# A linear-attention and MLP kernel: scores, masks and state updates of two chunks made side by side, in a new order of all steps

## The chip, the cores and the metric

The kernel runs on one core of a Trainium2 chip. The metric is the device time of one execution in microseconds (us), the median of several runs. A core has five engines that run side by side, each with its own list of instructions: TensorE (PE, with its weight loads shown as PEld), VectorE (DVE), ScalarE (ACT), GpSimd (POOL) and SyncE (SP), which here issues all the transfers. Engines wait for each other on semaphores. PE writes to PSUM, of which this kernel uses eight banks; everything else lies in SBUF.

## The reference

A recurrence over 768 tokens, for 4 batches of 8 heads of 48 channels, then a two-layer MLP with hardswish on the 3072 x 384 result.

```python
for t in range(S):                       # S = 768; state is B x H x 48 x 48
    state = alpha[:, :, t, :, None] * state + np.einsum('bhd,bhe->bhde', k[:, :, t], v[:, :, t])
    y[:, :, t] = np.einsum('bhd,bhde->bhe', q[:, :, t], state)
...
x = attn_out.transpose(0, 2, 1, 3).reshape(B * S, H * D)      # 3072 x 384
h = x @ w_in                                                  # 384 x 2048
relu6 = np.clip(h + 3.0, 0.0, 6.0)
g = h * relu6 / 6.0
return (g @ w_out).astype(np.float32)                         # 2048 x 384
```

The two weight matrices come as float64 and are turned to float32 on the chip.

## The kernel before

**Attention.** The tokens are cut into 24 chunks of 128, six for each batch. The 8 heads of a chunk lie as 4 pairs of two. A chunk goes through these steps, each with a short name that the order below uses, and a chunk number behind it:

- `la`, `lk`, `lq`, `lv` load alpha, k, q and v (L248, L271). `ta`, `tk`, `tq` turn them to channels by tokens: for chunks 0 to 5 on PE through PSUM (L282), from chunk 6 on with a DVE transpose of 32x32 blocks (L286); `ca` places alpha.
- `r` (L309, a scan, with the reciprocal of L313) is the product of the alphas from a token to the end of the chunk, `p` (L320) its counterpart from the start. `k` and `q` multiply by them (L332, DVE).
- `sc` (scores, L338 to L346) makes k by q in 32 matmuls: for each of 4 pairs, 2 halves of the chunk and 2 heads, a block of 64x64. The heads with a = 0 go to one PSUM bank, those with a = 1 to another, each using 256 of the bank's 512 columns. `m` (masked, L348 to L356) multiplies them by a triangular mask into the tile A: four DVE operations of 64x256. `qa` (L366, ACT) puts q itself into the other rows of A.
- `kb` and `ck` bring k back to tokens by channels: on PE up to chunk 7, later by a DVE transpose (`kt`, L391) and a trip through DRAM (`kw`, `kr`).
- `u` (update, L423 to L429) makes k by v in 32 matmuls (16 in a batch's last chunk), one PSUM bank for each half, 192 columns used. `sm` (L437, L439, DVE) adds it to the state; `st` (L409, POOL) decays the state; `sv` (L419, ACT) puts it into rows of v, so that `ya` and `yb` (attend, L455, 32 matmuls a chunk in 64 records) give masked scores by v and q by state added in one go. `cy` (L464, ACT) copies the result to xT.

**MLP.** Two chunks make a group of 256 tokens. Groups 0 and 1 run plain: first layer `f`, `fa`, `fb` (L478, L489), gate `fr` (ACT), hidden value `fg` (DVE), second layer `b` (L516). Groups 2 to 11 run with fewer products and more sums: `xc` (DVE) makes combinations of x, `M` (L600) 20 products, `n` (L606, ACT) keeps some of them, `o` (L537, L539, L541, DVE) adds them up, `e` (L494, ACT) and `h` (L498, DVE) make the hardswish; `s` (L647, L664, DVE) combines hidden values, `P` (L703) are seven products, `K` (ACT) keeps some, `G` (L719, DVE) adds up, `O` stores. `x` and `y` make the combinations of the weights that these products need.

**Weights.** 16 slices of 128x768: `w` loads one, `d1`, `d2`, `dx` (ACT), `d3` (DVE; L203 and L205, or L207, L208 and L210) and `d4` (POOL, L217) take the float64 words apart and together again.

**Idle fill.** `z` (L532) are matmuls on nothing needed, 29 in all.

**What sets the order.** Everything stands in one list of words in `run("""...""")` under a manual schedule: `sc.4.0.2` is scores of chunk 4 in the banks t0 and t2, `M.2.0.2` product 0 of group 2 in bank m2. Each engine, and SP with its transfers, executes its share of the list in that order; where two words meet in a bank or a tile, the later waits. There are four banks t0 to t3 for attention and four m0 to m3 for the MLP. The tiles A (two, by the parity of the chunk) and the quads, in which chunks from 6 on are loaded, are allocated once; the parts of the quads that no transfer fills are set by small POOL memsets (L257) in the loads of chunks 6 and 7.

The lines for A, the pads, the masks and the updates before:

```python
t = consts.tile([C, 2, H, HB], FP, tag=f"A{r}", name=f"A{r}")              # one for r = 0, one for r = 1
...
if j < FIRST + NQ:                                                          # in load_akq
    for o in (BLK, 3 * BLK):
        nc.gpsimd.memset(to[o : o + BLK, :, V - 1, D - BLK : BLK], 1.0)
```

Of the kernel before, what the change touches and what calls it, by code (L numbers as in the profile page):

```python
# [8 lines left out]
FP = mybir.dt.float32  # L9
# [4 lines left out]
ALU = mybir.AluOpType  # L14
# [3 lines left out]
def kernel(  # L18
# [42 lines left out]
    G = 2  # L61
# [32 lines left out]
    for r in range(NV):  # L94
        t = consts.tile([C, 2, H, 64], FP, tag=f"v{r}", name=f"v{r}")
        nc.gpsimd.memset(t, 0.0)
        vs.append(t)
    for r in range(2):
        t = consts.tile([C, 2, H, HB], FP, tag=f"A{r}", name=f"A{r}")
        nc.gpsimd.memset(t, 0.0)  # L100
        As.append(t)
# [145 lines left out]

    def load_akq(name, j):  # L248
# [6 lines left out]
        if j < FIRST + NQ:  # L255
            for o in (BLK, 3 * BLK):
                nc.gpsimd.memset(to[o : o + BLK, :, V - 1, D - BLK : BLK], 1.0)  # L257
# [80 lines left out]
    def scores(j, *at):  # L338
        sc = ps_t["sc", j] = [banks[i][:, 0 : NP * HB].rearrange("s (p t) -> s p t", p=NP)
# [28 lines left out]
    def last(j):  # L368
        return j % NC == NC - 1
# [52 lines left out]
    def update(j, *at):  # L422
        for b, i in enumerate(at):  # L423
            ps_t["u", j, b] = banks[i][:, 0 : NP * D].rearrange("r (p n) -> r p n", p=NP)
# [296 lines left out]
    def store2(g, i):  # L721
# [8 lines left out]
        "lq": lambda j: load_akq("q", j), "lv": load_v, "w": load_weight,  # L730
# [4 lines left out]
        "sc": scores, "m": masked, "qa": place_q, "kb": k_by_token, "ck": keep_k,  # L735
# [9 lines left out]
    def run(words):  # L745
        for word in words.split():
            name, *at = word.split(".")
            steps[name](*(int(x) for x in at))

    with tc.manual_schedule():  # L750
        run("""z.0.5 z.0.3 z.0.1 z.0.8 qa.0.0 w.0 d2.0 d3.0 la.0 ta.0.0 ca.0 r.0 lk.0 tk.0.1 k.0
               z.0.2 p.0 la.1 ta.1.2 lq.0 tq.0.3 ca.1 r.1 lk.1 lv.0.0 sv.0.0 d1.0 kb.0.0 ck.0 z.0.2
               u.0.2.1 sm.0.0 sv.0.1 q.0 qa.0.1 tk.1.0 k.1 p.1 z.0.2 sc.0.2.3 m.0 la.2 ta.2.0 ca.2
               dx.0 w.2 d2.2 kb.1.0 ck.1 lq.1 r.2 sm.0.1 st.1 tq.1.2 q.1 d3.2 z.0.3 d1.2 dx.2 lv.1.1
               u.1.3.1 sv.1.0 sm.1.0 p.2 sm.1.1 sc.1.0.2 m.1 ya.0.3 yb.0 cy.0 lq.2 w.1 d1.1 tq.2.1
               q.2 d4.2 lk.2 tk.2.3 k.2 fa.2.0 d4.0 st.2 sc.2.0.2 d2.1 d3.1 m.2 dx.1 d4.1 qa.1.1
               lk.3 la.3 ta.3.1 ca.3 la.4 fa.0.1 sv.1.1 w.3 r.3 ta.4.3 ca.4 r.4 tk.3.1 k.3 kb.2.0
               qa.1.0 d2.3 ya.1.2 yb.1 cy.1 fa.1.2 lq.3 ck.2 d1.3 p.3 d3.3 lv.2.2 u.2.3.2 sm.2.0
               d4.3 fb.2 tq.3.1 q.3 fb.1 qa.2.0 sm.2.1 sv.2.0 st.3 fr.0.2.0 fg.0.2 lk.4 tk.4.0
               sv.2.1 w.5 d2.5 k.4 d3.5 d1.5 qa.3.0 d4.5 qa.2.1 sc.3.1.3 m.3 w.6 d2.6 d1.6 d3.6 d4.6  # L760
               lv.3.0 lq.4 w.7 kb.3.2 fb.0 f.0.3.3 kb.4.0 ya.2.1 ck.3 u.3.3.2 sm.3.0 fr.0.3.1 fg.0.3
               fr.0.1.0 fg.0.1 qa.3.1 sv.3.0 sm.3.1 p.4 d2.7 sv.3.1 d1.7 d3.7 d4.7 f.0.5.0 fr.0.5.1
               fr.0.0.0 fg.0.5 fg.0.0 tq.4.3 ck.4 la.5 ta.5.2 f.0.6.3 ca.5 w.4 d2.4 ya.3.0 yb.3 cy.3
               fr.0.6.1 yb.2 cy.2 w.9 d2.9 q.4 qa.4.1 d1.4 d1.9 dx.4 la.6 w.8 d3.4 r.5 lk.5 w.10
               d3.9 p.5 ca.6 fg.0.6 d4.9 w.12 lq.5 lv.4.1 d2.8 d3.8 f.0.7.2 d1.8 st.4 d4.8 d4.4 w.11
               fr.0.7.0 fg.0.7 f.1.7.0 fr.1.7.1 fg.1.7 sc.4.0.2 m.4 f.1.1.1 fr.1.1.0 fg.1.1 f.1.3.3
               fr.1.3.1 d2.10 d1.10 tk.5.3 f.1.0.2 d2.12 d3.10 d4.10 w.13 fg.1.3 fr.1.0.0 fg.1.0 k.5
               d3.12 lq.6 f.1.6.0 f.1.2.1 u.4.1.0 sm.4.0 d1.12 d4.12 sv.4.0 qa.4.0 ya.4.2 fr.1.6.1
               fg.1.6 w.15 tq.5.3 fa.4.3 sv.4.1 d2.11 kb.5.1 d2.13 fr.1.2.0 f.1.4.2 fr.1.4.1 d1.11
               sm.4.1 q.5 r.6 d3.11 d3.13 fg.1.4 d4.11 lv.5.0 lk.6 tq.6 p.6 d2.15 d3.15 fg.1.2 d1.13  # L770
               d4.13 sc.5.0.3 yb.4 f.1.5.0 fr.1.5.1 fg.1.5 tk.6 m.5 b.1.0.2 fb.4 b.1.1 d1.15 d4.15
               st.5 y.5 w.14 la.7 lk.7 cy.4 d2.14 qa.5.1 ck.5 b.0.0.1 fr.0.4.0 d3.14 k.6 q.6 ca.7
               fg.0.4 d1.14 d4.14 x.0 y.1 y.10 b.0.1 y.0 y.2 u.5.2 P.1.0.0 K.1.0 qa.5.0 sv.5.0
               qa.6.1 P.1.1.3 b.0.2 b.1.2 kb.6.0 ya.5.3 y.6 s.1.0.0 sm.5.0 sv.5.1 G.1.0.0 tk.7
               s.1.1.1 s.1.2.3 x.1 yb.5 cy.5 b.1.3 sc.6.1.2 lv.6.2 ck.6 u.6.3.0 s.1.3.2 x.2 P.1.2
               b.0.3 K.1.1 y.7 s.1.4 s.1.5 y.11 y.3 r.7 xc.2.1 x.3 y.4 y.8 xc.2.3 k.7 xc.2.0 xc.2.4
               y.9 y.12 y.16 y.13 y.15 P.1.3.3 K.1.2 P.1.4 bo.1 P.1.5 xc.2.5 G.1.1.1 P.1.6 y.14 y.17
               y.19 xc.2.6 sm.6.0 G.1.2.2 y.20 M.2.0.2 lv.12.1 la.8 O.1.1 O.1.0 ca.8 y.18 y.21 y.23
               so.1 G.1.3.3 n.2.0.8 bo.0 lq.7 lv.7.0 O.1.2 m.6 xc.2.2 xc.2.10 xc.2.7 tq.7 r.8 p.7
# [153 lines left out]
```

## Time and profile before

| | us |
|---|---|
| median of 3 runs (533.48 to 533.62) | 533.5 |
| the profiled execution | 533.84 |
| its span, from the first to the last record | 531.8 |
| granted TensorE clock, mean | 1.00 |
| busy: PE, DVE, ACT, POOL | 522.2, 477.0, 257.4, 50.4 |

The profile is that of one execution. The 2.0 us by which its time exceeds the span lie around what the profiler records. The costliest groups on PE are the products of the second layer (L703: 121.7 + 91.5 us in 1232 records) and of the first (L600), on ACT the copies of L606 (63.6 us) and the gates of L494 (56.8 us), on DVE the hidden values of L498 (53.7 us in 80) and the sums of L537. The masks (L356) are 96 operations on DVE with 36.0 us, 0.413 each by duration. A row of the page or a view has: line, engine, operation, output and input, shape; then count, busy time and the mean of one. A matmul of float32 has more than one record.

### The profile page before, as it was taken

What the parts mean: (1) busy time and instruction counts of PE and PEld (TensorE: products, weight loads), DVE (VectorE), ACT (ScalarE), POOL (GpSimd) and SP (SyncE); (2) the same over time, 40 slices, a digit from 0 to 9 for tenths busy, and PEclk for the clock granted to TensorE, in tenths of its full rate; (3) what the DMA queues carried; (4) which work ended last, traced back from release to release, by engine and by line L of the source; (5) the groups of instructions that cost most, each with busy time, mean ns of one, the idle gap of its engine ahead of it and who ended that gap; (6) DMA issues with size and microseconds to landing.
All of it is one profiled execution on the core that took longest, in us unless ns stands there. A gap on an engine that the chain in (4) does not pass through costs nothing.

```text
span 531.8 us, 15143 instructions
## 1 busy us (share of the span) xinstructions
PE 522.2 (98%) x6306; PEld 496.9 (93%) x6306; DVE 477.0 (90%) x849; ACT 257.4 (48%) x503; POOL 50.4 (9%) x71
## 2 busy tenths in 40 slices
PE   7799999999999999999999999999999999999997
PEld 7698886789999999999999999999999999999997
DVE  6999989999999999999999999999999899496382
ACT  3889865212653553553544444642634544553340
POOL 5333425100000000000000000000000000000000
PEclk9999999999999999999999999999999999999999
DMA  9998887006615156254345356055364052100001
GB/s 173 218 254 247 211 231 156 18 2 149 155 31 118 30 125 139 49 137 100 89 107 118 90 123 143 18 134 111 92 138 105 10 110 44 44 2 2 15 16 37
DMA packets 124100, 54.40 MB, mean 102 GB/s; under 512 B 83328, under 2 KB 116864, under 8 KB 124032
## 3 DMA queue, kind: packets, MB, share of 16 engines
q1 hardware_dynamic: 124032, 53.44, 44.0%
q8 instruction: 49, 0.80, 0.7%
q14 instruction: 19, 0.16, 0.1%
HBM read 44.50 MB, written 8.91 MB: 100 GB/s over the span
## 4 chain that ended last, share of the span: by engine, by line
PE 81%; DVE 9%; ACT 3%; DMA 3%; POOL 2%; issue 1%; SPq 0%; DVEq 0%; POOLq 0%; ACTq 0%
PE m_ps L703 34%; PE m_ps L600 34%; PE m_ps L478 4%; PE t_ps L455 3%; PE t_ps L346 2%; PE t_ps L429 2%; DMA v<-in_v_dram 1%; DMA raw<-in_moe_w_out_dram 1%; DVE rings L647 1%; DVE R L309 1%; DVE raw L537 1%; ACT raw L186 1%; DVE g_sb L647 1%; ACT raw L191 1%; DVE w L537 1%
## 5 line engine op out<-in xcount | busy, mean ns | idle before, releaser
L606 ACT COPY g_sb<-m_ps 128x512 f32<-128x512 f32 x110 | 63.6, 584 | 123.7 <-PE m_ps L600 104.3
L703 PE MATMUL m_ps<-w,g_sb 128*128 128x192 f32 x704 | 121.7, 327 | 0.0
L703 PEld LDWEIGHTS m_ps<-w,g_sb 128*128 128x128 f32 x704 | 113.7, 190 | 0.4
L703 PE MATMUL m_ps<-rings,g_sb 128*128 128x192 f32 x528 | 91.5, 326 | 0.0
L703 PEld LDWEIGHTS m_ps<-rings,g_sb 128*128 128x128 f32 x528 | 85.4, 190 | 0.1
L600 PE MATMUL m_ps<-xc,w 128*128 128x128 f32 x640 | 82.8, 277 | 0.4 <-DVE w L541 0.4
L600 PEld LDWEIGHTS m_ps<-xc,w 128*128 128x128 f32 x640 | 77.5, 192 | 1.7 <-issue 0.6
L494 ACT ACTIVATE r<-g_sb,half 128x512 f32<-128x512 f32 x80 | 56.8, 722 | 33.1 <-DVE g_sb L541 12.1
L498 DVE SCALAR_TENSOR_TENSOR g_sb<-r,g_sb 128x512 f32<-128x512 f32 x80 | 53.7, 683 | 4.3 <-ACT r L494 3.9
L600 PE MATMUL m_ps<-xT,raw 128*128 128x128 f32 x400 | 52.5, 277 | 0.0
L600 PEld LDWEIGHTS m_ps<-xT,raw 128*128 128x128 f32 x400 | 48.6, 192 | 0.6
L409 POOL TENSOR_TENSOR st<-sm,R 128x192 f32<-128x192 f32 x20 | 12.9, 643 | 352.2 <-DVE sm L439 305.5
L647 DVE TENSOR_TENSOR g_sb<-g_sb 128x512 f32<-128x512 f32 (+1 forms) x55 | 41.9, 792 | 0.2
L600 PE MATMUL m_ps<-xT,w 128*128 128x128 f32 x320 | 42.0, 276 | 0.0
L600 PEld LDWEIGHTS m_ps<-xT,w 128*128 128x128 f32 x320 | 39.3, 192 | 0.1
L366 ACT COPY A<-q 48x256 f32<-48x256 f32 x88 | 35.6, 404 | 5.0 <-DVE q L332 3.8
L356 DVE TENSOR_TENSOR A<-t_ps,mask 64x256 f32<-64x256 f32 x96 | 36.0, 413 | 0.4
L478 PE MATMUL m_ps<-xT,w 128*128 128x256 f32 x144 | 32.8, 382 | 0.1
L600 PE MATMUL m_ps<-xc,raw 128*128 128x128 f32 x240 | 31.8, 276 | 0.0
L309 DVE TENSOR_TENSOR_SCAN R<-t,ones 128x516 f32<-128x516 f32 x24 | 29.6, 1235 | 1.0 <-ACT t L300 0.9
L478 PEld LDWEIGHTS m_ps<-xT,w 128*128 128x128 f32 x144 | 26.7, 190 | 3.8 <-POOL w L217 0.2
L600 PEld LDWEIGHTS m_ps<-xc,raw 128*128 128x128 f32 x240 | 29.6, 192 | 0.1
(104 smaller groups left out, 725.8 us busy)
## 6 DMA issues: line engine op xcount, KB each, us to landing
raw<-in_moe_w_out_dram SPq DMA_DIRECT2D x8, 768.0 KB, 5.3
raw<-in_moe_w_in_dram SPq DMA_DIRECT2D x6, 768.0 KB, 6.6
v<-in_v_dram SPq DMA_DIRECT2D x48, 96.0 KB, 3.1
out_dram<-oh SPq DMA_DIRECT2D x44, 96.0 KB, 1.7
far<-kq SPq DMA_DIRECT2D x64, 64.0 KB, 2.2
kb<-far SPq DMA_DIRECT2D x64, 64.0 KB, 2.1
aq<-in_alpha_dram SPq DMA_DIRECT2D x36, 96.0 KB, 2.7
qq<-in_q_dram SPq DMA_DIRECT2D x36, 96.0 KB, 2.5
```

The costliest lines, as they stand in the source:

```text
L309: nc.vector.tensor_tensor_scan(out=reverse(R, n - 1, n), data0=reverse(ax, n, n), data1=reverse(ones, n, n), initial=0.0, op0=ALU.mult, op ...
L356: nc.vector.tensor_tensor(out=to[:, a], in0=sc[a][half], in1=mask[half, half].unsqueeze(1).to_broadcast([HB, NP, HB]), op=ALU.mult)
L366: nc.scalar.copy(out=to[:, a], in_=Q_t[j][64 * a : 64 * a + D, :, half])
L409: nc.gpsimd.tensor_tensor(out=st, in0=sm, in1=R_t[j][:, :, 0:1].to_broadcast([C, NP, D]), op=ALU.mult)
L455: nc.tensor.matmul(y_of(j, (i + 1) // 2, p)[:, HB * b : HB * b + HB], vb[:, p, e : e + 32], A_t[j][:, b, 2 * p + a], start=(b == 0 and i = ...
L478: nc.tensor.matmul(h[:, f], w1[:, kk, o : o + C], xT_t[g][:, kk], start=(kk == 0), stop=(kk == KT - 1))
L494: nc.scalar.activation(out=to, in_=h, func=AF.Relu, bias=half, scale=1.0 / 6.0)
L498: nc.vector.scalar_tensor_tensor(out=to, in0=r, scalar=1.0, in1=h, op0=ALU.min, op1=ALU.mult)
L600: nc.tensor.matmul(acc[g][i][:, f * C : (f + 1) * C], spots[w][:, f * C : (f + 1) * C], x_of(g, x), start=(first and f == 0), stop=last, s ...
L606: nc.scalar.copy(out=slots[z], in_=acc[g][i])
L647: nc.vector.tensor_tensor(out=out, in0=in0, in1=in1, op=ALU.subtract)
L703: nc.tensor.matmul(to[g], a, rhs[:, f], start=(first and f == 0), stop=(last and f == HF - 1), skip_group_check=True)
```

## The change

From chunk 8 on (chunks 8 and 9, 10 and 11, ... 22 and 23) three steps take two chunks at a time:

- `sp` (scores_of_two) makes the scores of j and j + 1 in the same two banks: chunk j in columns 0 to 255, j + 1 in columns 256 to 511. The matmuls are the same.
- `mp` (masked_two) masks both with four DVE operations of 64x512 in place of eight of 64x256. For that the two tiles A become one tile `both`, whose two parts are still called As[0] and As[1].
- `up` (update_two) makes the updates of both chunks in the same banks, j in columns 0 to 191, j + 1 in columns 192 to 383. The matmuls are the same; the sums `sm` still go chunk by chunk.

Besides, the memsets on the quads leave `load_akq` and become a word of their own, `pd` (two of them, six memsets each), which stands near the beginning of the list. And the whole list of words is new: the place of nearly every step, and the bank that it uses.

```diff
+    both = consts.tile([C, 2, 2, H, HB], FP, tag="A", name="A")
     for r in range(2):
-        t = consts.tile([C, 2, H, HB], FP, tag=f"A{r}", name=f"A{r}")
-        nc.gpsimd.memset(t, 0.0)
-        As.append(t)
+        nc.gpsimd.memset(both[:, :, r], 0.0)
+        As.append(both[:, :, r])
...
+    def pad(r):
+        for name in "akq":
+            for o in (BLK, 3 * BLK):
+                nc.gpsimd.memset(quads[name, r][o : o + BLK, :, V - 1, D - BLK : BLK], 1.0)
...
-        if j < FIRST + NQ:
-            for o in (BLK, 3 * BLK):
-                nc.gpsimd.memset(to[o : o + BLK, :, V - 1, D - BLK : BLK], 1.0)
...
-    def scores(j, *at):
-        sc = ps_t["sc", j] = [banks[i][:, 0 : NP * HB].rearrange("s (p t) -> s p t", p=NP)
+    def scores_of_two(j, *at):
+        for c in range(2):
+            scores(j + c, *at, o=c * NP * HB)
+        ps_t["sp", j] = [banks[i] for i in at]
+
+    def masked_two(j):
+        sc = ps_t.pop(("sp", j))
+        for c in (j, j + 1):
+            A_t[c] = As[c % 2]
+        for b in range(2):
+            half = slice(HB * b, HB * b + HB)
+            to = both[half, b].rearrange("s c (p a) t -> s a (c p) t", a=2)
+            for a in range(2):
+                nc.vector.tensor_tensor(
+                    out=to[:, a], in0=sc[a][half].rearrange("s (n t) -> s n t", t=HB),
+                    in1=mask[half, half].unsqueeze(1).to_broadcast([HB, 2 * NP, HB]), op=ALU.mult)
+
+    def scores(j, *at, o=0):
+        sc = ps_t["sc", j] = [banks[i][:, o : o + NP * HB].rearrange("s (p t) -> s p t", p=NP)
...
+    def update_two(j, *at):
+        update(j, *at)
+        update(j + 1, *at[0 : 1 if last(j + 1) else 2], o=NP * D)
+
-    def update(j, *at):
+    def update(j, *at, o=0):
         for b, i in enumerate(at):
-            ps_t["u", j, b] = banks[i][:, 0 : NP * D].rearrange("r (p n) -> r p n", p=NP)
+            ps_t["u", j, b] = banks[i][:, o : o + NP * D].rearrange("r (p n) -> r p n", p=NP)
```

The two lists at their beginning:

```diff
-        run("""z.0.5 z.0.3 z.0.1 z.0.8 qa.0.0 w.0 d2.0 d3.0 la.0 ta.0.0 ca.0 r.0 lk.0 tk.0.1 k.0
-               z.0.2 p.0 la.1 ta.1.2 lq.0 tq.0.3 ca.1 r.1 lk.1 lv.0.0 sv.0.0 d1.0 kb.0.0 ck.0 z.0.2
+        run("""w.0 z.0.5 la.0 la.1 lk.1 z.1.8 lk.0 d2.0 lq.0 d1.0 d3.0 pd.1 ta.0.0 w.1 z.1.1 ca.0
+               z.0.3 pd.0 lv.0.0 dx.0 r.0 sv.0.0 z.1.3 la.2 p.0 z.0.2 w.2 tk.0.0 ta.1.1 lq.1 k.0
+               d4.0 tq.0.2 ca.1 z.0.3 q.0 tk.1.1 qa.0.1 kb.0.2 r.1 z.0.2 ck.0 lv.1.1 sc.0.0.3 d2.1
...
```

By instructions: DVE 849 before and 817 after (96 masks of 64x256 become 32 of 64x256 and 32 of 64x512), PE's matmuls, ACT's 503, POOL's 71 and the 472 transfers on SP are the same in number.

## The prediction, made before the changed kernel ran

> **What bounds the kernel now.** I read the first two parts of the page, then the chain by engine, the windows, and last the chain and the timelines where I wanted one price.
>
> ```profile
> PE 522.2 (98%) x6306; PEld 496.9 (93%) x6306; DVE 477.0 (90%) x849; ACT 257.4 (48%) x503; POOL 50.4 (9%) x71
> ...
> PE   7799999999999999999999999999999999999997
> ...
> DVE  6999989999999999999999999999999899496382
> ...
> PE 81%; DVE 9%; ACT 3%; DMA 3%; POOL 2%; issue 1%; SPq 0%; DVEq 0%; POOLq 0%; ACTq 0%
> ```
>
> PE looks full everywhere, but the records of small matmuls stretch over waits, so the windows say more (after the length: PE, PEld, DVE, ACT, POOL).
>
> ```profile
> 0.00:25.00 25.00, 18.97 (x289) 16.54 (x289) 19.91 (x40) 14.88 (x21) 9.80 (x23) 1.00 1.11 198
> 25.00:70.00 45.00, 44.69 (x580) 39.44 (x581) 44.06 (x71) 41.11 (x70) 19.13 (x17) 1.00 0.89 229
> 70.00:110.00 40.00, 40.00 (x430) 29.89 (x430) 38.33 (x53) 16.66 (x30) 10.33 (x15) 1.00 0.49 121
> 110.00:160.00 50.00, 49.58 (x557) 47.51 (x558) 49.32 (x93) 21.40 (x44) 1.00 (x1) 1.00 0.39 90
> 160.00:270.00 110.00, 110.00 (x1453) 108.19 (x1452) 105.38 (x195) 50.41 (x106) 3.46 (x6) 1.00 0.44 97
> ```
>
> From 25 to 160 us DVE is busy 44.06 of 45, 38.33 of 40 and 49.32 of 50 us, while the weight loads, which stop when PE stops, fall to 29.89 of 40: PE is the one that waits. From 160 on DVE has 4.6 us idle in 110 and PEld runs on. So there are two stages: up to about 156 us DVE sets the time (ACT beside it from 25 to 70, 41.11 of 45), afterwards PE alone.
>
> To say how far each engine is behind, I summed for every place in the list of words the work that stands ahead of it on its engine, one operation priced by the distance to the next start where it runs without a wait. That makes PE's work 504.9 us in all and DVE's 467.1. "Late" below is the time of a place less the work ahead of it. The last product that waits for DVE is word P.2.1.3 at 156.2 us: PE has 138.4 us of work behind it (17.8 late), DVE must have done 143.4 (12.4 late). Of PE's 23.6 us at the end only 5.8 arise later.
>
> **Fewer changes between large and small matmuls on PE.** The change pulls scores and updates of a pair together on PE. The chain around one such place, before:
>
> ```profile
> 178.09 0.89 PE m_ps L600 x8
> 178.98 0.62 PE t_ps L346 x32
> 179.61 0.51 PE t_ps L429 x31
> 180.12 3.77 PE m_ps L600 x32
> 183.88 1.92 PE t_ps L455 x128
> 185.81 1.98 PE m_ps L600 x16
> ...
> 193.89 1.78 PE m_ps L600 x16
> ```
>
> Sixteen records of L600 take 1.78 us inside a row of products and 1.98 behind an attention block: 0.20. The block that stands first (L346, 32 records) takes 0.62, the one behind it, about as many records, 0.51: 0.11. One excursion costs 0.31 us. Counting runs of L346, L429 and L455 in the PE order of the two lists gives 43 before and 36 after. Behind 136 us of PE work, where PE is the bound, it is 25 and 16: 9 x 0.31 = 2.8 us on the path. The seven by which the other part differs (18 before, 20 after) lie under DVE and cost nothing; if PE set that part too, 0.6. Bounds: the 0.20 alone, 1.8; and 0.33 each, the largest such excess in this chain by single records, 3.0. I take **-2.8**.
>
> The Trainium skill, page "TensorEngine Tiling (Array Packing)", section "Key Properties", says that TensorE drains when the tile size changes. The rows agree, with 0.31 us for there and back; the sum goes by them.
>
> **Masks two chunks wide.** Eight pairs lose 8 operations of 64x256 and gain 4 of 64x512.
>
> ```profile
> 175.92 1.52 DVE L356 TENSOR_TENSOR A<-t_ps,mask 64x256 f32<-64x256 f32 x4
> 177.47 0.36 DVE L439 TENSOR_TENSOR sm<-t_ps,s 128x192 f32<-128x192 f32 x1
> ...
> 178.34 0.68 DVE L537 TENSOR_TENSOR g_sb<-m_ps,g_sb 128x512 f32<-128x512 f32 x1
> 178.95 0.70 DVE L391 STREAM_TRANSPOSE kq<-k 128x512 f32<-128x512 f32 x1
> ```
>
> Four old masks take 1.52 us, 1.39 from start to start once the overlap is taken off (0.348 each). 64x512 does not occur; its neighbour 128x512 out of PSUM takes 0.61 to the next start. Lower bound 0.35 (no dearer than half the size), upper 0.70 (no gain); I take 0.615, the row with the same elements per partition. A pair saves 8 x 0.348 - 4 x 0.615 = 0.32 us, all of them 2.6. Only pair 8/9 falls before the end of DVE's stage: **-0.3** there, the other 2.3 hide under PE, which sets the time from there on (if DVE did, they would count: see rival 3). The mask of the first chunk now waits for the scores of the second, 0.5 us; what stands behind it on DVE are sums that PE reads later. The new list leaves about 7 us of PE work between a pair's updates and its first attend, which covers the wait; without cover it would be 8 x 0.5 = 4 us. Updates in one bank need no new instruction: 704 matmuls before and after, as all counts other than the masks (POOL 71, ACT 503, 472 transfers on SP).
>
> **The pads.** Twelve memsets on POOL (L257, 2.3 us together) go from chunks 6 and 7 to the front, in two words. POOL is busy 9.80 of the first 25 us and waits there for DVE's weight words; cost nothing, and if the first sums of weights (L217) stood behind them, up to 2.3 on POOL only. SP no longer has any wait on them.
>
> **The start.** Transfers on SP are put as w.0, la.0, la.1, lk.1, lk.0, lq.0, w.1, where before w.0 was followed by la.0, lk.0, la.1, lq.0, lk.1. With about 1.2 us from landing to landing as in the trace (la.0 6.9, lk.0 8.2, la.1 9.4), k of chunk 0 comes 2.3 us later, but the transposes of alpha for chunk 1 and the first weights come earlier in the engines' lists. Following the new words by hand with the rows' durations, the first half-product fa is reached at 20.7 us (24.9 before) and word fb.2 with DVE 5.5 us late instead of 6.6, PE 10.0 instead of 12.6. In DVE's stage the DVE figure counts: **-1.1** (bounds 0 and -2.6). DVE also had one idle wait of 1.14 us at 71 us, for an update of chunk 4; in the new list that state sum stands later behind its update. I give half: **-0.6**.
>
> **POOL beside DVE.** Here the list can take time back.
>
> ```profile
> 81.32 1.18 DVE L320 TENSOR_TENSOR_SCAN P<-t 128x516 f32<-128x516 f32 x1
> 82.40 1.77 DVE L207 TENSOR_SCALAR w<-w 128x768 f32<-128x768 f32 x1
> ...
> 92.69 1.96 DVE L332 TENSOR_TENSOR q<-q,P 128x512 f32<-128x512 f32 x1
> ```
>
> ```profile
> 81.73 2.02 POOL L217 TENSOR_TENSOR w<-raw 128x768 int32<-128x768 int32 x1 [0.17 <-POOL kq L257]
> ...
> 92.40 1.69 POOL L217 TENSOR_TENSOR w<-raw 128x768 int32<-128x768 int32 x1 [3.73 <-DVE raw L210]
> ```
>
> L332 takes 0.68 elsewhere and 1.96 when L217 began 0.3 us before it; L207 1.77 against 0.61. Both end with the POOL operation. Adding up such excesses before gives 3.2 us, all ahead of 100 us. In the new list each L217 starts just behind its L210, and I looked which DVE word follows: nine times (weights 2, 4, 5, 6, 8, 10 and 13, one r, one xc) it is one that has been seen held; with what remains of the 1.5 us of an L217 that is 6.2 us. Bounds 0 and +3.0 more than before; I take half, **+1.5**.
>
> The Trainium skill, page "SBUF — State Buffer", section "Who interferes with whom", says that a DVE instruction with two SBUF inputs, or in a mode that uses both ports, shuts out a GpSimd one that reads SBUF, and the other way round, for the whole instruction. The two rows agree; by the page the nine places would cost their full +3.0, which is rival two.
>
> **The sum.** At PE work 136.1 the new list (word P.2.1.2) needs 142.3 us of DVE work, 6.2 ahead, where the old one needed 5.0. DVE then is 12.4 - 1.1 - 0.6 + 1.5 = 12.2 late (the mask's 0.3 is inside the 142.3), so it comes at 154.5 us. Before, PE was at that work at 153.6: +0.9. With the -2.8 that is -1.9. Own time 533.84 (span 531.8 and 2.0 around it) becomes 531.9; the median of the runs is 0.3 below its profiled execution, so **531.6**.
>
> **Rivals.**
> 1. *The DVE stage gives way altogether* (locks rare, the start as walked on PE: 10.0 late instead of 12.6). Then -2.6 - 2.8 = -5.4: **528.1**. For it: the start is DMA-bound, and 42 fewer wait instructions on DVE (207 to 165); against: 98% busy DVE up to 160.
> 2. *The locks take the gain*: +1.5 more, -0.4: **533.1**, no difference.
> 3. *The tie to DVE lasts to 270 us of PE work*: slower. In the old list the lead that PE's products need of DVE falls from 5.0 at 138 us of PE work by steps to about 1 at 270 and below 0 after 280; in the new one it stays at 5.3 to 6.2 up to P.5.0.3 (PE 251.3, DVE 257.5). So each wait of DVE there, for ACT's copies or for PE, goes on the path. If the 4.6 us idle of 160 to 270 remain, DVE is 12.2 + 4.6 = 16.8 late, P.5.0.3 starts at 274.3, PE 23.0 late instead of 20.0: +3.0; behind it 16 excursions become 10, -1.9: 534.6. Where PE waits for DVE, DVE's own waits for PE come later too; with half as much idle again (an estimate) it is +2.3, 536.9. I price it at **535.6**, in the middle. It decides from 3.5 us of DVE idle time in that stretch: the whole change is that idle time less 3.5. Against it: a DVE that is needed sooner also has its inputs sooner, as ACT is half idle from 70 on.
> 4. *The pairs do nothing* (wide masks at 0.70): 0.3 + 0.0 of DVE, inside the first case.
>
> **Chances.** Forecast, 530.3 to 532.4: 0.37; rival 1: 0.14; rival 2: 0.20; rival 3: 0.29. A measurement of this kernel tells 0.2% (1.07 us) from nothing: faster 0.50, same 0.21, slower 0.29. The range goes from 528.6 to 536.3; the likeliest case's own is 530.3 to 532.4.
>
> **What would show it.** Right: L600 blocks without the 0.2 behind them at 16 places after 156 us, DVE at full load until about 155 and then with idle time, L356 64x512 at 0.68 recorded. The start: fa near 21 us. Wrong: L207, L309 or L332 over 1.2 us beside L217 more than four times (rival 2); PE gaps behind DVE words, PEld under 107 in 160 to 270 (rival 3); PE at P.2.1 before 152 us (rival 1). A score block that waits for a transfer would be none of these.

## The result, and the profile after

| | before | after |
|---|---|---|
| median of the runs, us | 533.56 (533.48 to 533.83) | 542.34 (541.30 to 542.61) |
| the same two kernels in a later comparison | 533.80 (533.68 to 534.28) | 541.80 (539.72 to 542.33) |
| the profiled execution shown, and its span | 533.84, 531.8 | 542.33, 540.6 |

The changed kernel is slower: the ratio is 1.0157 with an interval of 1.0137 to 1.0177, and 1.0142 (1.0120 to 1.0163) the second time. The forecast was 531.6, so it is 10 us off and on the wrong side. The first profiled execution of the changed kernel took 888.89 us at a mean granted clock of 0.56 and is left out of the figures above; the profile after is that of another execution, from the second comparison.

The first two parts of the page after, and the chain by engine:

```profile
PE 523.8 (97%) x6306; PEld 498.2 (92%) x6306; DVE 480.4 (89%) x817; ACT 260.4 (48%) x503; POOL 52.5 (10%) x71
...
PE   8789989999999999999999999999999999999997
...
DVE  6988999999999999999999899799999999376291
...
PE 78%; DVE 12%; SPq 4%; DMA 3%; issue 2%; ACT 0%; DVEq 0%
```

The counts are as the diff says (DVE 817). PE has slices of 7 and 8 among the first seven, where before only the first two were short of 9. The sums of busy time differ by 1.6 us on PE and 3.4 on DVE; where 8.8 us arise, the windows say (after the length: PE, PEld, DVE, ACT, POOL, then the clock):

```profile
0.00:25.00 25.00, 19.76 (x278) 18.05 (x279) 20.34 (x36) 16.64 (x21) 15.45 (x36) 1.00 1.06 202
25.00:70.00 45.00, 40.06 (x598) 34.12 (x597) 40.81 (x63) 35.74 (x64) 10.27 (x10) 0.96 0.96 228
70.00:110.00 40.00, 37.27 (x332) 28.66 (x333) 39.15 (x58) 19.34 (x32) 14.15 (x11) 1.00 0.61 154
110.00:160.00 50.00, 49.94 (x556) 45.12 (x555) 49.68 (x87) 18.76 (x41) 2.12 (x2) 1.00 0.27 65
160.00:270.00 110.00, 110.00 (x1432) 108.82 (x1434) 108.45 (x188) 52.71 (x108) 3.42 (x6) 1.00 0.48 109
```

From 25 to 70 us every engine is less busy than before: the weight loads 34.12 (39.44 before), DVE 40.81 (44.06), ACT 35.74 (41.11). In the next two windows PE's loads are short once more (28.66 for 29.89, 45.12 for 47.51), and from 160 us on they run as before (108.82 for 108.19). So the time is lost ahead of 160 us. One word in the chain after dates it: the product P.2.1.2, which the prediction put at 154.5 us, starts at 162.27.

```profile
155.80 1.09 PE m_ps L623 x8
156.89 2.60 PE m_ps L726 x16
159.49 2.78 PE m_ps L623 x24
162.27 2.74 PE m_ps L726 x16
```

From there to the end it is 378.3 us; before, with the same 136.1 us of PE work done at 153.6, it was 378.2. The word has 142.3 us of DVE work ahead, so PE is 26.2 late there and DVE 20.0. Word by word, the difference to the old list grows early: at 20, 30, 40, 50 and 70 us of DVE work DVE is 7.8, 8.4, 12.7, 15.5 and 18.3 us late (before 5.7, 6.9, 7.6, 7.7 and 9.0), and at 130 us 19.4 (12.2). Two kinds of rows make that up. First, DVE operations that stand beside L217 on POOL. From the timeline of DVE, then that of POOL (start, duration):

```profile
20.93 2.07 DVE L203 TENSOR_SCALAR w<-w 128x768 f32<-128x768 f32 x1
...
63.51 2.56 DVE L322 TENSOR_TENSOR_SCAN P<-t 128x516 f32<-128x516 f32 x1
...
70.62 1.23 DVE L207 TENSOR_SCALAR w<-w 128x768 f32<-128x768 f32 x1
```

```profile
19.80 2.65 POOL L217 TENSOR_TENSOR w<-w,raw 128x768 int32<-128x768 int32 x1 [0.76 <-DVE w L205]
...
63.13 1.85 POOL L217 TENSOR_TENSOR w<-w,g_sb 128x768 int32<-128x768 int32 x1 [4.28 <-ACT g_sb L191]
69.98 1.46 POOL L217 TENSOR_TENSOR w<-raw 128x768 int32<-128x768 int32 x1 [5.00 <-DMA aq<-in_alpha_dram]
```

L203 takes 0.78 alone and 2.07 here, the scan L322 1.22 and 2.56, L207 0.55 and 1.23; they end 0.4 to 1.1 us behind POOL's operation. Summed over 5 to 160 us such excess is 8.9 us (3.9 before, counted alike; the prediction had 3.2). Second, waits of DVE:

```profile
41.82 0.69 DVE L207 TENSOR_SCALAR w<-w 128x768 f32<-128x768 f32 x1 [2.42 <-ACT w L196]
...
46.07 0.78 DVE L207 TENSOR_SCALAR w<-w 128x768 f32<-128x768 f32 x1 [0.97 <-ACT w L196]
```

In the new list ACT's words for weight 5 stand behind the gate fr.0.2.0, which waits for PE's half-product fb.2:

```profile
40.31 0.69 ACT L517 ACTIVATE r<-m_ps,half 128x512 f32<-128x512 f32 x1 [4.63 <-PE m_ps L512]
40.89 0.90 ACT L196 ACTIVATE w<-raw 128x768 f32<-128x768 f32 x1
```

ACT sat still for 4.63 us and DVE behind it for 2.42, although the raw words of weight 5 were there at 36.45. Not all of that is the order's. PE itself came late with fb.2: it stood still for 1.62 us from 34.36 us on, waiting for nothing that the profile shows, and then ran fb.2 at half clock (last section). The variant with single masks (544.60 below) has the same words up to here and the gap too, but its trace has the full clock at this place: there ACT waits 3.12 us, and the two waits of DVE come to 1.8 us in place of 3.4, so about half of the 3.4 goes with the half clock.

The weight loads show the delay, since a load waits until L217 has freed its raw slot. Those of the second layer from 58 to 92 us, before, then after (minimum, median and maximum duration, first and last start):

```profile
L166 SPq DMA_DIRECT2D raw<-in_moe_w_out_dram x5: 367/385/419, 59.6 to 81.2; - x5
```

```profile
L166 SPq DMA_DIRECT2D raw<-in_moe_w_out_dram x6: 373/385/574, 58.9 to 90.1; - x6
```

The last is issued at 90.1 us for 81.2. Slice 12, the first in the row before, goes at 71.5 for 59.6.

### The profile page after: what moved, and what is told of

The parts are those of the page before. It is cut to its first block, busy times and chain, and to the rows that moved or that the text cites. A ratio compares the mean times of both kernels' runs of the same rounds, so it can differ in the third digit from the quotient of the medians.

```text
span 887.1 us, 15093 instructions
## 1 busy us (share of the span) xinstructions
PE 882.5 (99%) x6306; PEld 745.3 (84%) x6306; DVE 485.2 (55%) x817; ACT 263.1 (30%) x503; POOL 51.0 (6%) x71
## 4 chain that ended last, share of the span: by engine, by line
PE 99%; ACT 0%; POOL 0%; issue 0%; POOLq 0%
PE m_ps L726 40%; PE m_ps L623 35%; PE m_ps L501 6%; PE t_ps L478 4%; PE m_ps L539 4%; PE t_ps L365 2%; PE m_ps L512 2%; PE t_ps L452 2%; PE t_ps L284 2%; PE m_ps L555 1%; PE t_ps L393 1%; ACT t L302 0%; ACT oh L739 0%; POOL ident masks.py:199 0%; ACT v L438 0%
## 5 line engine op out<-in xcount | busy, mean ns | idle before, releaser
L726 PE MATMUL m_ps<-w,g_sb 128*128 128x192 f32 x704 | 210.6, 486 | 0.0
L726 PEld LDWEIGHTS m_ps<-w,g_sb 128*128 128x128 f32 x704 | 159.0, 232 | 38.2 <-issue 0.8
L726 PE MATMUL m_ps<-rings,g_sb 128*128 128x192 f32 x528 | 158.8, 486 | 0.0
L726 PEld LDWEIGHTS m_ps<-rings,g_sb 128*128 128x128 f32 x528 | 119.9, 234 | 28.4 <-issue 0.4
L629 ACT COPY g_sb<-m_ps 128x512 f32<-128x512 f32 x110 | 64.4, 585 | 254.6 <-PE m_ps L623 215.6
L623 PE MATMUL m_ps<-xc,w 128*128 128x128 f32 x640 | 135.7, 386 | 0.0
L623 PEld LDWEIGHTS m_ps<-xc,w 128*128 128x128 f32 x640 | 127.5, 273 | 5.5 <-issue 1.1
L623 PE MATMUL m_ps<-xT,raw 128*128 128x128 f32 x400 | 85.5, 387 | 0.0
L623 PEld LDWEIGHTS m_ps<-xT,raw 128*128 128x128 f32 x400 | 81.4, 280 | 2.1
L623 PE MATMUL m_ps<-xT,w 128*128 128x128 f32 x320 | 67.8, 389 | 0.0
L623 PEld LDWEIGHTS m_ps<-xT,w 128*128 128x128 f32 x320 | 64.6, 293 | 0.9
L670 DVE TENSOR_TENSOR g_sb<-g_sb 128x512 f32<-128x512 f32 (+1 forms) x55 | 42.4, 796 | 21.5 <-PE m_ps L726 19.8
L623 PE MATMUL m_ps<-xc,raw 128*128 128x128 f32 x240 | 51.8, 391 | 0.0
L623 PEld LDWEIGHTS m_ps<-xc,raw 128*128 128x128 f32 x240 | 49.1, 278 | 1.6
L501 PEld LDWEIGHTS m_ps<-xT,w 128*128 128x128 f32 x144 | 31.8, 226 | 20.8 <-issue 12.4
L478 PEld LDWEIGHTS t_ps<-A,v 128*32 128x32 f32 x1536 | 34.5, 137 | 7.4 <-issue 4.5
```

The costliest lines, as they stand in the source:

```text
L478: nc.tensor.matmul(y_of(j, (i + 1) // 2, p)[:, HB * b : HB * b + HB], vb[:, p, e : e + 32], A_t[j][:, b, 2 * p + a], start=(b == 0 and i = ...
L501: nc.tensor.matmul(h[:, f], w1[:, kk, o : o + C], xT_t[g][:, kk], start=(kk == 0), stop=(kk == KT - 1))
L623: nc.tensor.matmul(acc[g][i][:, f * C : (f + 1) * C], spots[w][:, f * C : (f + 1) * C], x_of(g, x), start=(first and f == 0), stop=last, s ...
L629: nc.scalar.copy(out=slots[z], in_=acc[g][i])
L670: nc.vector.tensor_tensor(out=out, in0=in0, in1=in1, op=ALU.subtract)
L726: nc.tensor.matmul(to[g], a, rhs[:, f], start=(first and f == 0), stop=(last and f == HF - 1), skip_group_check=True)
```

## The experiments

The changed kernel was also run beside the first of its variants; its figure there (541.8) is the one that they are compared with. The kernel before took 533.6 to 534.1 us beside each group of them.

> The changed kernel as it is, for a profile at full clock: its first profiled execution ran at a granted clock of 0.56, while the three others took 541.3 to 542.6 us at 0.997. By rival 3 (the tie to DVE lasts) the loss lies between 140 and 290 us, with PEld under 107 us of the 110 between 160 and 270. By rival 2 (POOL beside DVE) it lies before 110 us, with L207, L332 or L309 over 1.2 us beside L217. A third case: the clock is granted below 1.0 in one stretch, and the loss is there. About 542 us in each case.

**Which part of the list loses the time.** Four kernels take one list up to a word and the other from there on. Words to be made twice or not at all by that are left out or put in, and four banks are renamed at the seam.

Before's list up to M.3.3 (159 us), then the changed order with its pairs:

```diff
-w.0 z.0.5 la.0 la.1 lk.1 z.1.8 lk.0 d2.0 lq.0
...
+z.0.5 z.0.3 z.0.1 z.0.8 qa.0.0 w.0 d2.0 d3.0 la.0
...
 M.3.3
...
```

> The list of before up to its word M.3.3 (159 us, no pair yet), then all other words in the order of the changed kernel, pairs included; four banks renamed where a value still lies. If the whole loss comes from the start: 530.5 to 534, from -2.6 us for 16 excursions in place of 25, given back in part by small waits. If pairs and the later order cost by themselves: 536 or above.

Measured: 535.03 (534.16 to 535.39), ratio 1.0020 (1.0011 to 1.0029). Behind before's start the part with the pairs costs 1.3 us, seam included; it doesn't gain 2.8.

The reverse, the changed list up to M.3.3 and then before's words, without a pair:

> The reverse: the list of the changed kernel up to M.3.3 (167 us), then the words of before, chunk by chunk, no pairs. If the start carries the loss: 540 to 544. If pairs do: 533 to 536.

Measured: 544.31 (543.05 to 544.87). The loss stays with the start, and the part behind the seam is 2.5 us worse than with the pairs. The two directions don't add up (7 us of loss from the first, 10.6 from the second); perhaps before's second part stands a late DVE less well than the new one, which no run shows.

Before's list up to sm.2.1 (38 us), and up to m.4 (65 us), then the changed order:

> The list of before only up to its word sm.2.1 (38 us), then the changed kernel's order. DVE is 1.5 us later there in the changed kernel, and 9 us later by 75 us. If the loss arises behind that point (weight pieces on ACT, DVE and POOL, and their loads): 537 to 542. If a late beginning is multiplied by what follows: 532 to 535.

> The list of before up to its word m.4 (65 us, weights 0 to 9 and 12 on their way), then the changed kernel's order. If the loss arises up to there, 531 to 534.5; if loads of chunks 6 to 8 ahead of the last weights cost by themselves, 535 to 539.

Measured: 538.55 (538.31 to 539.65) and 545.15 (544.37 to 547.01). The first gives a ledger of the 8.1 us: 541.8 - 538.55 = 3.2 in the first 38 us, 538.55 - 535.03 = 3.5 from there to 159 us, 1.3 behind. As the two directions above don't add up, these are shares for exchanges made from the front, not prices of the parts. The second is a miss: it is slower than the changed kernel, its trace has long waits that neither list has by itself (DVE 7.2 us for gates and 3.4 for one update between 60 and 110 us) and three stretches at half clock (mean 0.984), so it says nothing of 38 to 65 us.

**The wide masks undone.** The pairs stay, each chunk is masked by itself:

```diff
     def masked_two(j):
-        sc = ps_t.pop(("sp", j))
...
+        ps_t.pop(("sp", j))
+        masked(j)
+        masked(j + 1)
```

> The changed kernel with its list and banks, but each pair's masks made chunk by chunk, 8 operations of 64x256 in place of 4 of 64x512. If the wide masks save DVE 0.32 us a pair and DVE still sets the time up to 290 us (rival 3), up to 5 of the 8 pairs count: 1 to 2 us slower than the changed kernel. If the wide masks are themselves what costs (64x512 over 0.85 us recorded), it is faster than the changed kernel. If DVE sets nothing after 156 us: the same within 0.5 us.

Measured: 544.60 (543.54 to 545.92), ratio 1.0206 (1.0185 to 1.0227): 2.8 us slower than the changed kernel. The rows after have the sizes that were forecast:

```profile
L353 DVE TENSOR_TENSOR A<-t_ps,mask 64x512 f32<-64x512 f32 x32 | 20.6, 681 | 0.1
...
L375 DVE TENSOR_TENSOR A<-t_ps,mask 64x256 f32<-64x256 f32 x32 | 12.0, 414 | 0.2
```

In the trace with single masks PE waits, behind 155 us, 1.1 us for masks and 0.6 for a state that DVE makes; in the changed kernel it waits for neither. So the wide masks do what they are for, and in this order about all of the 2.6 us of DVE work that they save counts, not 0.3.

**POOL's sums of the weight words taken away.** In both kernels L217 becomes a memset of the weights (and one of a single raw word, for the order), which leaves out adding the low words: the weights are zero.

```diff
-        nc.gpsimd.tensor_tensor(out=dst.bitcast(I32), in0=high.bitcast(I32),
-                                in1=lo.bitcast(I32), op=ALU.add)
+        nc.gpsimd.memset(dst, 0.0)
+        nc.gpsimd.memset(lo[:, 0:1, 0:1], 0)
```

> The changed kernel in which POOL's sums of weight words (d4, L217 before) are left out: a memset of the same tile stands in their place, so the weights are zero and the order, the banks and the waits stay. In the changed kernel's profile DVE operations that run beside a d4 take 7.9 us more than their usual time, before 94 us. If that is on the path (theory: DVE, slowed by POOL, sets the start), 535 to 537 us, 5 to 7 under the changed kernel. If the start is set by the loads and by ACT's queue instead, at most 2 us under it.

> The kernel before with the same left out, d4's sums, a memset in their place. The excess beside d4 is 3.1 us there. If the theory holds, 530.5 to 531.5 us, and the gap between the two kernels shrinks from 8.0 us by 3 to 4.5. If the start is set otherwise, no faster than 533.

Measured: 537.18 (536.28 to 541.51), ratio 1.0086 (1.0048 to 1.0123), and 532.94 (532.58 to 533.52), ratio 0.9985 (0.9975 to 0.9994). By the medians the sums cost 4.6 us in the new list and 0.8 in the old. But the five runs of the first lie apart (536.28, 536.65, 537.18, 540.38, 541.51), and the trace is that of the last. In it the holds are gone, DVE is busy 94.01 us up to 110 us (100.30 in the changed kernel), and still PE's loads from 110 to 160 us are 45.46 (45.12). PE has a gap of 2.71 us there, up to 53.21 us, that waits for no engine, and a stretch at half clock behind it. So the gain isn't in every run, and no trace shows where it comes from. The memset is also shorter and frees the raw slot sooner, so this alone doesn't part the hold on DVE from the ring of slots (the slots for raw weights, each loaded again when its sum is done).

**The waits and the holds moved out of the way.** ACT's words for weights 5 and 6 ahead of the gate that held them:

```diff
-fb.0 fr.0.2.0 la.6 d2.5 fb.1 k.4 d1.5 d4.3
+fb.0 d2.5 d1.5 fr.0.2.0 d2.6 la.6 fb.1 k.4 d4.3
```

> The changed kernel with ACT's pieces of weights 5 and 6 (d2.5, d1.5, d2.6) moved ahead of, or right behind, the gate fr.0.2.0, on which ACT waits for PE while w.5 has long landed. DVE waits 2.4 and 1.0 us for these pieces at 41.8 and 46.1 us. If those waits are on the path: 2.4 to 3.4 us under the changed kernel, 538.5 to 539.5. If DVE only meets the next lock or load earlier: the same within 0.7.

Measured: 541.10 (540.16 to 543.35). The two waits of 3.4 us are gone, one of 0.8 ahead of a mask is new, and the time is 0.7 lower, within the spread.

The load lq.1 ahead of w.2, since PE waited for it at 19.57 to 21.25 us:

```diff
-la.2 p.0 z.0.2 w.2 tk.0.0 ta.1.1 lq.1 k.0
+la.2 p.0 z.0.2 lq.1 w.2 tk.0.0 ta.1.1 k.0
```

> The changed kernel with the load of q for chunk 1 put ahead of the load of weight 2, so that it lands near 17.5 us instead of 21.1. PE waits 1.7 us for it (tq.1.2 at 21.25). If PE's wait is on the path, 1 to 2 us under the changed kernel; if DVE, held in d3.2 until 23.7 us, sets that place, the same within 0.5.

Measured: 544.74 (543.18 to 546.66), slower; in the profiled execution (546.66) the mean clock is 0.991, with stretches at half clock from 21.6 and 38.7 us. A miss: moving q ahead of the weight brings nothing, and how much of the loss is the clock's isn't parted.

Words of DVE moved so that scans and weight words no longer stand beside L217 (the edit above among them):

```diff
-p.2 qa.1.1
-sc.1.2.3 sm.1.1 d4.2 k.2
+k.2 sm.1.1
...
-w.10 p.5
+fg.0.6 p.5
...
-d4.10 sm.4.1
+fg.1.3 sm.4.1
...
```

> The changed kernel with the same work, and only the order of words on DVE and ACT in the first 90 us changed: behind each weight slice's last DVE operation stands one that POOL's sum did not hold up (from PSUM, or a block transpose), and d2.5, d1.5, d2.6 are early as before. If locks beside d4 and ACT's queue make the loss at the start, the excess of DVE beside POOL falls from 8.9 us to about 3.5 and the time to 535.5 to 537.5. If the leaving out of d4 gained for another reason (weights free earlier, loads earlier), at most 1.5 us under the changed kernel.

Measured: 542.91 (542.01 to 545.06): no gain. Its windows say why:

```profile
0.00:25.00 25.00, 20.35 (x267) 18.77 (x267) 18.38 (x34) 17.63 (x24) 15.46 (x36) 0.93 1.04 200
25.00:70.00 45.00, 40.61 (x622) 35.32 (x615) 41.98 (x68) 35.70 (x64) 12.76 (x10) 1.00 1.01 231
70.00:110.00 40.00, 35.67 (x327) 27.15 (x326) 34.61 (x54) 18.51 (x30) 12.29 (x10) 1.00 0.60 152
110.00:160.00 50.00, 49.98 (x556) 45.17 (x555) 49.41 (x87) 18.85 (x41) 1.93 (x2) 1.00 0.27 65
```

DVE is busy 94.97 us up to 110 us where the changed kernel has 100.30. The 5.3 us taken off come back as idle time, and PE's loads from 110 to 160 us are 45.17 as against 45.12.

The loads of chunks 5 to 8 behind those of the weights (first below), and both edits together:

```diff
-d3.4 d1.4 la.7 qa.4.0
+d3.4 d1.4 qa.4.0
...
-kb.5.3 w.14 b.0.1
+kb.5.3 w.14 la.7 lq.7 la.8 lk.8 b.0.1
...
```

> The changed kernel with only SP's order changed from weight 10 on: loads of chunks 5 to 8 that nothing reads before 95 us (v of 5, k of 7, q of 6, a and q of 7, a and k of 8) go behind weights 11 to 14. In the changed kernel la.8 holds SP's queue from 63.1 to 67.8 us until DVE is done with ca.6, and w.12 behind it is issued at 71.5 (59.6 before). Theory now: two limits lie close together in the start, DVE slowed by POOL and the ring of weight slots (load, d3, d4, next load). Then this alone brings little, 0 to 2 us under the changed kernel. If the loads alone set the start: 535 to 538.

> The same order of loads, together with the order of DVE and ACT words that took most of the excess beside POOL away (8.9 to 2.5 us) without a gain, and with ca.6 left early. If two limits lie close together, taking both away gains what neither does: 535 to 538. If neither is the limit, 541 or more, as the changed kernel.

Measured: 541.55 (540.06 to 542.10) and 541.33 (539.96 to 541.51). Neither differs from 541.8 by more than its spread. The same kind of edit on the kernel with before's first 38 us:

> The kernel with before's first 38 us and the changed order behind it (538.55 us), with DVE's words moved as in e7 where POOL's sums hold them up (d3.4, d3.6, d3.10, d3.13, r.6): 3 to 3.5 of its 6.6 us of excess should go. Here DVE hardly waits (5.3 us, before 5.0) and the clock is full. If DVE's excess beside POOL is what 38 to 95 us cost: 535.5 to 537. If, as in e7, waits for loads and ACT take its place: 538 or above.

Measured: 540.52 (539.14 to 541.92) where 538.55 stood without it, with DVE busy 3.6 us less from 25 to 110 us. Here too the excess removed became waits, and the time rose by 2.0.

**A fourth slot for raw weights**, in the kernel of 541.33. It lies in the part of w2 that slices 14 and 15 fill last; the raw words of slice 14 move to a slot that also takes two sums of first-layer weights, so slice 14 isn't what the reference has.

```diff
+    raws.append(w2[:, 12:16].rearrange("p f n -> p (f n)").bitcast(U32).rearrange(
+        "p (n w) -> p n w", w=2))
-    HOMES = [0, 1, 2, 3, 4, 0, 1, 2] + [(i + 3) % 3 for i in range(NW - NW1)]
+    HOMES = [0, 1, 2, 3, 4, 0, 1, 2] + [0, 1, 2, 1, 5, 0, 1, 2]
```

> The changed kernel with loads and DVE words moved as in the run before of that kind (541.3), and a fourth place for raw weights from slice 12 on: 12 uses the part of w2 that slices 14 and 15 fill later, so 12 waits for no slice, 11 for 9, 13 for 8, 15 for 10, 14 for 11, each one slice earlier than before. Theory A (the ring of raw slots is what turns the removed excess beside POOL into DVE's waits for ACT's weight words): L166 loads of 12, 11, 13 and 15 are issued 5 us earlier, the two waits of L207 for ACT (2.1 us) go, 538.5 to 539.5 us. Theory B (the ring is not it; DVE's other waits, for the gates and for PE, and PE's own work in the order of the list set 38 to 95 us): the loads come earlier, the waits move to L521 and L462, 541 to 541.8 us.

Measured: 540.39 (540.19 to 541.94), ratio 1.0129 (1.0109 to 1.0149) against 1.0135: no difference. The loads did come earlier (weight 12 at 58.6 us in place of 68.5, the next at 68.2 in place of 73.1, then 72.7 for 77.1), and DVE's waits for weight words are what they were (DVE, then ACT; the sum, times, the longest):

```profile
DVE w L209 <- ACT w L198: 2.1, 2, 1.2
```

```profile
ACT r L519 <- DVE g_sb L523: 6.8, 4, 2.1
```

So the ring of raw slots isn't the limit there. Where the memset kernel has its gain from stays open: the ring alone isn't it by this run, nor the holds alone by those of 542.91 and 540.52. What does stand ahead of the weight words on ACT is a gate that waits for DVE: a gate needs one of two tiles r, which DVE's hidden value sets free. From 36 to 100 us ACT waits so, before and after the change:

```profile
ACT r L494 <- DVE g_sb L498: 1.6, 1, 1.6
```

```profile
ACT r L517 <- DVE g_sb L521: 7.1, 3, 3.8
```

A late DVE word delays a gate, the gate the weight words behind it on ACT, and these the next DVE word. That loop is seen, but no kernel took it apart (a third tile r), so it isn't shown that it sets these 57 us.

**Idle fill on PE**, three `z` words ahead of tq.1.2, tq.2.0 and ya.2.3, against the stretch at half clock:

```diff
-tq.1.2 cy.0
+z.3.5 tq.1.2 cy.0
...
-tq.2.0 w.3
+z.3.4 tq.2.0 w.3
...
-ya.2.3 la.5
+z.3.4 ya.2.3 la.5
```

> The changed kernel with 13 more fill matmuls on PE, 2.9 us, at three places where PE stands idle in the first 36 us (before tq.1.2, tq.2.0, ya.2.3). Each timed run of the changed kernel had one stretch of 3.4 us at half clock, which came behind an idle PE. If these stretches cost time, the granted clock goes to 1.0 and the time falls by 1 to 2 us; if they are hidden behind DVE, the clock rises and the time stays within 0.5; if the idle time is not what lowers the clock, neither changes.

Measured: 543.04 (541.13 to 543.86), with the clock at 1.00 in three runs of four. At 80 to 130 us of DVE work DVE is 16.6 late rather than 19.2 in the traced execution (541.13), but the fill itself is 2.9 us of PE work ahead of the same products. So the full clock alone doesn't bring the time back. A stretch of 3.41 us at half rate can cost 1.7 us at most; whether it does, and what the gap ahead of it costs, isn't parted by a run.

**The pairs alone, and the products that follow a copy.** Before's list with seven of the eight pairs, and the state sums and some words for k of later chunks moved to stand behind their pair:

```diff
-u.18.0.3 sc.18.1.2
...
-m.18
...
-sc.19.1.2 st.19 u.19.0.3
...
-sm.19.0 G.7.1.3 m.19 sv.19.1
+sp.18.1.2 up.18.0.3 sm.18.0 sm.18.1 sv.18.1
...
+sm.19.0 G.7.1.3 mp.18 sv.19.1
```

> The kernel before with its own list, in which only seven of the pairs (8/9 to 18/19 and 22/23) are made two at a time: scores and updates of the first chunk move to the second's place, the masks are four of 64x512, and what depends on them moves behind. If fewer excursions are worth 0.25 us each (6.2 us for 25 in the trace before) and nothing else comes in: 17 or 18 excursions, 531.5 to 532.2. If pairs bring waits of their own on banks, K and masks (in the changed kernel some 3 us of small steps appear on PE after 156 us): 533 or above.

Measured: 560.53 (559.87 to 561.14), ratio 1.0500 (1.0485 to 1.0516), PE's loads 102.83 of 110 from 160 to 270 us. Between 150 and 400 us PE waits 9.0 us for ACT's copies (L629), 2.4 for masks and 1.7 for such a copy ahead of an attend; in the old list, none of these. Most likely a pair made to wait for its second chunk pushes all that stands behind it; in any case the pairs need an order made for them, and this run says nothing of what they are worth in one.

In the kernel of 535.03, PE was followed from 159 us on. It loses 7.5 us over its work there, of which 16 excursions are 4.25. The rest is a wait for an update's k out of DRAM, a gap behind a product, and some 25 steps of 0.05 to 0.10 us at products that continue in a bank right after ACT has copied its contents:

```profile
304.53 2.87 PE L726 MATMUL m_ps<-w,g_sb 128*128 128x192 f32 x16 [0.47 <-issue]
```

```profile
367.28 0.57 PE L452 MATMUL t_ps<-v,kb 64*48 64x48 f32 x30 [0.65 <-DMA kb<-far]
```

In the new list 37 products have only one other (0.89 us) between them and the one whose result ACT copies (0.58 us); in the old one 8. A kernel that moves 18 products one place on, which leaves 5 such places of the 34 in this half, was to show that:

```diff
-M.3.5 s.2.2.15 s.2.1.11 P.2.3.3
+s.2.2.15 s.2.1.11 P.2.3.3 M.3.5
...
-M.3.19 n.3.10.14 o.3.6.0 M.3.11
+n.3.10.14 o.3.6.0 M.3.11 M.3.19
...
```

> The kernel with before's start and the changed order behind it (535.0 us), with PE's products moved: where a product that goes on in the bank of an earlier one follows it with a single product (0.89 us) between, while ACT copies that bank out (0.58 us and the way there and back), one more product is put between. 34 such places become 5; before has 8 in all. PE shows 0.05 to 0.10 us at most of them. If they give back the gain of the fewer excursions: 533 to 534. If they are harmless: 535.0 within 0.4.

Measured: 553.77 (553.35 to 554.00), 18.7 us slower, and PE falls behind all the way:

```profile
160.00:270.00 110.00, 106.18 (x1444) 103.58 (x1444) 104.28 (x178) 50.39 (x108) 3.67 (x6) 1.00 0.48 109
270.00:400.00 130.00, 123.35 (x1563) 119.48 (x1562) 116.52 (x206) 58.70 (x123) 4.45 (x6) 1.00 0.41 93
```

Between 150 and 400 us PE waits 7.5 us, in 11 places, for ACT's copies out of banks that it needs next (none in the kernel of 535.03), and DVE is busy 104.28 of 110 us where it had 108.85. Most likely a product moved back by one place makes the copy of its bank late, and all behind it; that costs far more than the steps. The steps stand as an account of the trace, not as shown by a run.

No kernel here that does the whole work beats before (the one of 532.94 leaves out the sums of the weights); the best that keeps the pairs is the one of 535.03.

## Why the prediction was wrong

The forecast span was 529.9 (531.9 less 2.0 around it), measured 540.6. Of the 10.7 us, 7.8 lie ahead of P.2.1.2 (162.27 for 154.5), 2.9 behind it (378.3 to the end for 375.4).

**The handover is the step that failed.** The prediction had DVE 12.2 us late there, from 12.4 - 1.1 - 0.6 + 1.5; it was 20.0.

- "POOL beside DVE", taken at +1.5 with +3.0 as the bound, measured +5.0 (8.9 in place of 3.9): 3.5 of the 7.8. Six of the nine places came (the weight words of slices 2, 4, 8, 10 and 13, and r.6), at 0.86 us each by duration less the time alone, where 6.2 for nine makes 0.69; slices 5 and 6 and the xc weren't held. The scans p.2 and p.5 (2.26 and 2.56), 2.4 us more, weren't among the nine. So the halving to +1.5 was wrong, and the bound too narrow: it took each L217 at 1.5 us, and L203 was held for 2.07 by one that itself took 2.65.
- The idle time, -0.6. The wait of 1.14 us for the update of chunk 4 did go, but the list has two new ones of 2.42 and 0.97 us, through the gate ahead of ACT's weight words: +2.3 in all, 2.9 off. The words were walked by hand on DVE and on PE up to fb.2, and ACT's queue behind it wasn't. About half of the two waits (3.4 against 1.8 us) goes with the half clock of this execution, if the comparison in the result holds; no term had that.
- The start, -1.1. fa comes at 21.72 us (20.7 forecast, 24.94 before), but at 30 us of its work DVE is 8.4 late (6.9 before), as L203 at 20.93 and p.2 at 24.87 are held. What is left for this term, once the two above are taken off, is 1.4 of the 7.8.

These are the sizes in the trace. Taking the terms away one at a time brought next to nothing back: 0.7 us for the two waits, nothing for the holds. So adding separate terms up, as the prediction did for the handover, isn't borne out by the runs either, and which of them sets the time stays open, as said below.

**The excursions, -2.8.** Right in place; in size (2.6 from the traces) partly by luck, as one costs 0.25 or less and not 0.31: before they make up all that PE loses behind 156 us, 25 of 0.25 (6.2 us), after it 16 of 0.22 (3.6). The chain after shows one: L623 takes 3.77 behind the update block and 3.62 in a row of products.

```profile
182.77 1.09 PE t_ps L365 x64
183.86 0.93 PE t_ps L452 x63
184.79 3.77 PE m_ps L623 x32
...
221.35 3.62 PE m_ps L623 x32
```

What was missed is that the new order gives all of it back, some 3 us, in waits and steps of its own, where the old list has none: 378.3 us from P.2.1.2 to the end for 378.2. The forecast put these at nothing and left them to rival 3. (The part ahead of it differs by two excursions, 18 and 20, not by the seven that the prediction names; its 0.6 is the price of two.)

**The masks, -0.3.** The duration (0.68) and the 2.6 us of DVE work were right, the cover was not: undone, they cost 2.8. DVE has 108.45 of 110 us full up to 270 us, so the 2.3 us that were to hide under PE show, as PE's waits for single masks do.

**The pads** at 0 were right as far as the trace says: POOL is busy 15.45 us of the first 25 (9.80 before), but the first L217 starts at 10.22 us, 0.3 us after the last ACT word that it needs (9.93), so they hold it up by that at most.

**The rivals.** Rival 1 didn't come. Rival 2, the locks: they came about as often as its sign asked (L207 at 1.23, 1.45 and 1.22, r at 2.01, besides L203 and the scans p), at a price far above its bound, which came from the same term; but no run shows that they alone make the loss. Rival 3 named the tie of PE to DVE from 160 to 270 us as the way to slower; the tie is there (DVE 19.8 to 21 us late throughout), but PEld is 108.82, not under 107, so DVE's waits there cost next to nothing. The loss arises before. No case put the whole start on the wrong side: its bounds went from 0 to a gain of 2.6, without a loss.

**Still open** is what sets 38 to 95 us of the new order. Holds beside POOL, ACT's waits for gate tiles and PE's waits are tied to each other; taking one away (541.1, 542.9, 541.6, 541.3, 540.4) moved the time to the next, and only leaving out the POOL sums gave 4.6 us by the median, in three runs of five. One rival was not tested by itself: PE's gaps that wait for no engine. In the old list the longest of them between 4 and 160 us is 0.95 us; the changed one has 1.62 us in the word ya.2.3, and the other kernels of the changed start have 0.8 to 2.7 us there.

## What to carry to other kernels

When a whole order is new, walk every engine's queue through the stage that sets the time, ACT's included: what stands behind an instruction that waits is late too, and a saving of instructions elsewhere is small beside it. Where operations on VectorE and GpSimd hold each other, price each place by the longest hold that the trace shows for either of the two, and give the start of a new order a bound on the side of a loss. A hold taken out of a stage in which engines wait in a loop can come back as a wait, as it did here; only a run tells. Look at which execution a trace is of before a gain of the median is read from it.

## What the runs showed of the hardware

The half clock. In the window from 33.5 to 36.9 us of the changed kernel PE has one gap, and the window behind it is at half clock:

```profile
33.50:36.90 3.40, 1.78 (x69) 1.30 (x68) 3.30 (x6) 2.16 (x3) 0.00 (x0) 1.00 1.13 278
36.90:40.30 3.40, 3.40 (x18) 3.40 (x18) 2.47 (x4) 0.00 (x0) 1.46 (x1) 0.50 1.07 364
```

```profile
33.18 0.60 PE L284 MATMUL t_ps<-ident,rings 128*128 128x128 f32 x4
33.71 0.65 PE L478 MATMUL t_ps<-A,v 128*32 128x64 f32 x28
35.98 0.31 PE L478 MATMUL t_ps<-A,v 128*32 128x64 f32 x4 [1.62 <-issue]
...
36.73 0.99 PE L284 MATMUL t_ps<-ident,rings 128*128 128x128 f32 x4
37.50 4.75 PE L512 MATMUL m_ps<-xT,w 128*128 128x128 f32 x29
```

The stretch lasts 3.41 us at a clock of 0.50: the four records of L284 at its edge take 0.99 us for 0.60. In their profiled executions the kernels of the changed start had one or more such stretches, at different places, all but the one with the fill (543.04); those with before's first 38 us had none, but for 545.15 and 560.53. Some timed runs of before have a mean clock of 0.997, as the changed kernel has, so it isn't free of them. The gap itself waits for no engine. One transfer of 16 KB on the instruction queue starts just ahead of it, between 33.5 and 34.0 us; nothing here shows whether the two are tied.

The Trainium skill, page "TensorE: Matmul & The Clock Gate", Part 1 on the HAM clock gate, gives a free-running window of 3413 ns and half rate after at least one idle window. The trace agrees with the length and the factor, but 1.62 us of idle time in a window of 3.40 was enough. It isn't always: with single masks (544.60) a gap of 1.66 us in the same word was followed by the full clock.

The scan with two inputs in SBUF is held by POOL's sum as L332 is: L322 2.56 us beside L217, 1.22 alone. The Trainium skill, page "SBUF — State Buffer", section "Who interferes with whom", says that a DVE instruction with two SBUF inputs contends with a GpSimd one that reads SBUF; these rows agree and put the scan among them.
